# Block products in the last MLP half, Silu gates, and work moved to GpSimd, in a clustered-attention and MLP kernel

## The chip, the core and the metric

The kernel runs on one core of a Trainium2 chip. A core has five engines, each with its own instruction queue that runs in order: TensorE (PE, matmuls and the loading of their weights), VectorE (DVE), ScalarE (ACT), GpSimd (POOL) and SyncE (SP, which issues DMAs here). They meet through semaphores. SBUF is the working memory; TensorE writes to PSUM, eight banks of 2 KB in each of 128 partitions, from where DVE or ACT take the results. The metric is the device time of one execution in microseconds (us).

## The reference: what is computed

```
scores = scale * q @ k^T                     # batch 4, heads 8, 768 tokens, head_dim 64
mask   = argmax(q_n @ c_n^T) == argmax(k_n @ c_n^T)    # 16 clusters per head
attn   = softmax(where(mask, scores, -1e9))
x      = (attn @ v), heads side by side      # 3072 tokens x 512
h      = x @ w_in                            # 512 -> 2048 features
out    = (h * sigmoid(h)) @ w_out            # 2048 -> 512
```

Every query and key gets the cluster whose centroid it points to most. A query sees only the keys of its own cluster. The result goes through an MLP with Silu gate.

## The kernel before

**Attention.** For one head a *job* holds six tiles of 128 queries and six of 128 keys. `load` fetches them as f32 (tile `raw`), `hi` (lines 123 to 127) rounds 128 times the value to f16, `lo` (L132) gives the rest as a second f16 half; the two stand side by side in `hl`. `xpose` turns them by DMA into `ab`, 64 rows high half and 64 rows low half. `logits_n` (L180) multiplies by the centroids into PSUM, `lsum` (L192) adds the two halves into an SBUF tile `L` that has two buffers, `mx_n` (L208) takes the largest of 16 clusters, and `ge_n` (L217) compares: the one-hot code. For the *late* jobs (heads 16 to 31 of 32) `c_scale` (L224, L225) makes of the ones 16384 on the queries' side, and of the zeros -16384 on the keys' side, on GpSimd. `c_xpose` and `c_move` (L237) bring the code by two DMAs into rows of `ab` below the high half, so that one matmul (`qk_mm`, L354) gives score and mask at once. `exp` (L359) makes the weights `P` on ACT. `pv` (L371) multiplies them with `vt` (values with a column of 2.0, whose sum serves for the division and halves the result), `norm` (L381, L383) divides, and the result is turned into `xt`, features by tokens.

**MLP.** Half a batch (384 tokens, named `(b, c)`) has 16 feature tiles. `unit_a` (L421) is four matmuls of 128 by 384; the result `ph` is h/2. ACT takes `tn = tanh(ph)` (L441) and DVE `gt = (tn + 1) * ph` (L444), which is h times sigmoid(h). After the last exp, `unit_a2` does two tiles at once (L467, L468) in the PSUM banks ("halls") that the scores used. The second matrix is applied either by `part_b` (L480) or, for pairs of token tiles, by class `Pair`: a two-by-two block multiplication with seven products in place of eight (L561), after four sums of activations (`sums`, L544) and with sums of weights made once (L514). Its results are put together out of PSUM (L567 to L604) and stored.

**Order.** The work up to about 38 us is a list written out by hand (`plan`). Behind it a planner in the same file runs: it keeps a clock for each engine with a length for every piece, and issues on each engine the piece that is next by due time. For TensorE it ranks scores, values, feature tiles and products; the rate of the scores is set by `PACE`, `LEAST`, `LESS`, `GAIN`. Dates count scores: `SPLIT` says at which score a head's split falls due, `AHEAD`, `VALUES` and `CAST` when its loads and its cast (L295) do. The planner only sets the order in the queues; on the chip, the semaphores decide. There are 192 scores (units); the last is number 191.

## Time and profile before

| | us |
|---|---|
| three runs: lowest, median, highest | 298.30, 299.58, 299.75 |
| profiled execution: first to last instruction (span) | 297.1 |
| PE, PEld, DVE busy | 288.0, 203.4, 219.7 |
| ACT, POOL busy | 221.7, 72.3 |

The profile gives the span of the one execution it recorded; that execution's own device time is not among its numbers, and the runs' median stands 2.5 us above the span. Busy time counts instructions on the engine, not the issuing of DMAs. Matmuls are pipelined and their ends are modelled, so a busy TensorE need not be one at its best. In the groups by line, the numbers behind the bar are busy us, mean ns of one, then the idle time of the engine just before and what ended it.

### The profile page before, as it was taken

The numbers are of one execution on the slowest core, as the hardware profiler recorded it, in microseconds if no ns is written. First come the engines' busy times: TensorE is split into PE (matmuls) and PEld (weight loads), VectorE is DVE, ScalarE is ACT, GpSimd is POOL, SyncE is SP. The second block draws the span as 40 slices with busy tenths as digits, with TensorE's granted clock in tenths as the row PEclk, the third lists the DMA queues.
The fourth block names the chain that finished last, engine by engine and source line by source line (L and its number), as shares of the span: only waits on it lengthen the run. The fifth ranks groups of instructions, "written<-read, shape, count | busy, mean of one in ns | idle before, by whom it ended". The sixth has DMA issues, their size and how long they took to land.

```text
span 297.1 us, 8186 instructions
## 1 busy us (share of the span) xinstructions
PE 288.0 (97%) x3273; PEld 203.4 (68%) x3273; DVE 219.7 (74%) x459; ACT 221.7 (75%) x365; POOL 72.3 (24%) x133
## 2 busy tenths in 40 slices
PE   7899799999999999999999999999999999999995
PEld 3786666566766566667766776678767786767783
DVE  5998559586897799997797766997664553569743
ACT  5899689765896579988579668997798879845410
POOL 2889510001031023544232560243200000000000
PEclk9999999999999999999999999999999999999999
DMA  6689999999866599999877979785220020110113
GB/s 208 206 244 204 158 257 228 170 235 185 242 128 174 133 214 227 209 223 196 232 175 144 196 215 226 170 126 119 74 57 17 13 86 15 49 38 0 35 38 141
DMA packets 77220, 44.61 MB, mean 150 GB/s; under 512 B 56288, under 2 KB 73088, under 8 KB 77184
## 3 DMA queue, kind: packets, MB, share of 16 engines
q1 hardware_dynamic: 71952, 35.55, 51.7%
q0 software_dynamic: 4800, 8.13, 15.0%
q8 instruction: 25, 0.41, 0.6%
q10 hardware_dynamic: 432, 0.43, 0.4%
q14 instruction: 11, 0.09, 0.1%
HBM read 27.30 MB, written 6.29 MB: 113 GB/s over the span
## 4 chain that ended last, share of the span: by engine, by line
PE 85%; DMA 7%; POOL 2%; DVE 2%; issue 1%; ACT 1%; SPq 0%; POOLq 0%; DVEq 0%; ACTq 0%
PE ph L421 28%; PE pS L354 18%; PE po L561 16%; PE pO L371 10%; PE po L480 9%; DMA raw<-in_q_dram 3%; PE psN L180 3%; DMA ab<-cd 3%; DMA ab<-cdt 1%; POOL hl L125 1%; DVE hl L132 1%; DVE ab L166 1%; POOL vt L295 1%; POOL win_s L613 0%; PE px L393 0%
## 5 line engine op out<-in xcount | busy, mean ns | idle before, releaser
L359 ACT ACTIVATE P<-pS 128x768 f16<-128x768 f32 x192 | 156.9, 826 | 36.9 <-PE pS L354 36.0
L421 PE MATMUL ph<-xt,win_s 128*128 128x384 f16 x512 | 97.6, 326 | 0.0
L354 PE MATMUL pS<-ab 128*128 128x384 f16 x384 | 93.2, 326 | 2.2 <-DMA ab<-cd 1.5
L444 DVE SCALAR_TENSOR_TENSOR gt<-tn,ph 128x384 f16<-128x384 f32 x110 | 58.7, 550 | 21.0 <-ACT tn L441 20.4
L421 PEld LDWEIGHTS <-win_s 128*128 128x128 f16 x512 | 49.3, 98 | 31.1
L441 ACT ACTIVATE tn<-ph 128x384 f32<-128x384 f32 x110 | 55.1, 514 | 3.3 <-PE ph L421 2.4
L354 PEld LDWEIGHTS <-ab 128*128 128x128 f16 x384 | 34.5, 98 | 20.8 <-issue 2.5
L371 PEld LDWEIGHTS <-P 128*128 128x128 f16 x1152 | 39.7, 97 | 5.0 <-DVE ab L166 0.9
L371 PE MATMUL pO<-vt,P 128*128 128x65 f16 x1152 | 41.2, 193 | 0.3 <-DVE ab L166 0.3
L132 DVE SCALAR_TENSOR_TENSOR hl<-raw,hl 128x768 f16<-128x768 f32 (+3 forms) x35 | 32.8, 939 | 1.2 <-POOL hl L125 0.5
L561 PEld LDWEIGHTS <-gt 128*128 128x128 f16 x304 | 29.3, 98 | 5.9 <-DVE gt L544 0.4
L480 PE MATMUL po<-wout_s,gt 128*128 128x512 f16 x128 | 32.5, 379 | 0.0
L295 POOL CAST vt<-vn 128x384 f16<-128x384 f32 x32 | 18.8, 598 | 56.2 <-DMA vn<-in_v_dram 40.7
L561 PE MATMUL po<-wout_s,gt 128*128 128x256 f16 x192 | 24.4, 273 | 0.0
L224 POOL TENSOR_SCALAR od<-od 128x96 f16<-128x96 f16 x16 | 9.3, 580 | 53.3 <-DVE od L217 53.2
L381 DVE RECIPROCAL zr<-pO 128x6 f32<-128x6 f32 x32 | 6.2, 193 | 18.9 <-PE pO L371 18.8
L180 PEld LDWEIGHTS <-ab 128*128 128x128 f16 x458 | 17.3, 97 | 4.0 <-DVE ab L166 0.3
L480 PEld LDWEIGHTS <-gt 128*128 128x128 f16 x128 | 12.0, 98 | 10.6
L383 DVE TENSOR_TENSOR xn<-pO,zr 128x384 f16<-128x384 f32 x32 | 17.8, 557 | 1.1
L180 PE MATMUL psN<-stk,ab 128*128 128x32 f16 (+1 forms) x458 | 18.6, 188 | 0.0
L561 PE MATMUL po<-tw,sg 128*128 128x256 f16 x128 | 16.3, 273 | 0.0
L192 DVE TENSOR_REDUCE L<-psN 128x192 f32<-128x384 f32 (+1 forms) x27 | 14.8, 549 | 1.9 <-PE psN L180 1.7
(101 smaller groups left out, 259.0 us busy)
## 6 DMA issues: line engine op xcount, KB each, us to landing
raw<-in_k_dram SPq DMA_DIRECT2D x31, 192.0 KB, 4.0
out_dram<-ot SPq DMA_DIRECT2D x23, 256.0 KB, 2.4
raw<-in_q_dram SPq DMA_DIRECT2D x24, 192.0 KB, 3.9
vn<-in_v_dram SPq DMA_DIRECT2D x16, 192.0 KB, 4.2
vn<-in_v_dram POOLq DMA_DIRECT2D x16, 192.0 KB, 4.3
win_s<-in_moe_w_in_dram POOLq DMA_DIRECT2D x8, 256.0 KB, 6.2
wout_s<-in_moe_w_out_dram POOLq DMA_DIRECT2D x4, 512.0 KB, 18.8
raw<-in_q_dram SPq DMA_DIRECT2D x2, 384.0 KB, 4.2
```

The costliest lines, as they stand in the source:

```text
L132: nc.vector.scalar_tensor_tensor(out=hl[:, s, 1, :], in0=raws[job.name][:, s, :], scalar=QS, in1=hl[:, s, 0, :], op0=ALU.mult, op1=ALU.sub ...
L180: nc.tensor.matmul(L[:, n % g, :, n // g], ab[:, i, :], stk[:, job.groups[i // 3][0], x : x + w], start=(x == 0), stop=(x + w == 2 * HC),)
L295: nc.gpsimd.tensor_copy(vt[:, :, 0:D], vns.pop(i))
L354: nc.tensor.matmul(pS[:, e, 0:HALF], abs_[kj.name][:, kn, :], rhs, start=True, stop=True)
L359: nc.scalar.activation(out=P, in_=pst.pop(u)[:, :, 0:HALF], func=AF.Exp, bias=0.0, scale=ESC)
L371: nc.tensor.matmul(o[:, (2 * t + h) * VW : (2 * t + h + 1) * VW], Ps[i + h, c, j // 2][:, j % 2, ts(t, 128)], vtb[(i + h) % 13][:, j, 0:VW ...
L383: nc.vector.tensor_tensor(out=xn, in0=ov[:, :, 0:D], in1=zr.unsqueeze(2).to_broadcast([128, 2 * NM, D]), op=ALU.mult)
L421: nc.tensor.matmul(ph[:, 0:HALF], win_s[:, r, ts(fb, 128)], xts[b, c][:, r, :], start=(r == 0), stop=(r == NR - 1))
L441: nc.scalar.activation(out=tn, in_=ph[:, 0:HALF], func=AF.Tanh, bias=0.0, scale=1.0)
L444: nc.vector.scalar_tensor_tensor(out=gt[:, fb, :], in0=tn, scalar=1.0, in1=ph[:, 0:HALF], op0=ALU.add, op1=ALU.mult)
L480: nc.tensor.matmul(po, gts[b, c][:, fc, ts(t, 128)], wout_s[:, fc, :], start=(fc == 0), stop=(fc == NFB - 1))
L561: nc.tensor.matmul(o, l[:, f, :], x, start=(f == 0 and k in begins), stop=(f == HK - 1), skip_group_check=True)
```

## The change

1. Of batch 3's two halves, the feature tiles 8 to 15 are no longer computed by `unit_a` but as two blocks of four tiles (class `Quad`), each by seven block products of four 192-column matmuls. Four sums of tokens per half (`x_sum`, DVE) and eight sums of weights (`t_piece`, GpSimd or DVE) go before; two copies out of PSUM (`copy`) and four additions (`plus`) go between the products of a block.
2. Behind the last exp, ACT loads the table of Silu. From there the gate is one Silu on ACT, without DVE.
3. For ten heads (`BY_GP`) `hi` runs on GpSimd rather than on DVE or ACT.
4. For late jobs the comparison is a subtraction on GpSimd, in place in `L`, and `c_scale` compares with zero and scales in one.
5. The last two pairs get two sum tiles more (`OWN`), so that the third and fourth sum no longer overwrite the activations.
6. New dates and pace constants, and rules for the order of the blocks among the plain tiles.

```diff
-        nc.vector.tensor_tensor(
-            out=ohv(job), in0=Ls.pop(job.name), in1=mx.unsqueeze(2).to_broadcast([128, g, HC, m]), op=ALU.is_ge
-        )
+        mx = mx.unsqueeze(2).to_broadcast([128, g, HC, m])
+        if job.late:
+            nc.gpsimd.tensor_tensor(out=Ls[job.name], in0=Ls[job.name], in1=mx, op=ALU.subtract)
+        else:
+            nc.vector.tensor_tensor(out=ohv(job), in0=Ls.pop(job.name), in1=mx, op=ALU.is_ge)
...
-        o = ohv(job)
-        nc.gpsimd.tensor_scalar(out=o[:, :, :, 0:3], in0=o[:, :, :, 0:3], scalar1=OHV, scalar2=None, op0=ALU.mult)
-        nc.gpsimd.tensor_scalar(
-            out=o[:, :, :, 3:6], in0=o[:, :, :, 3:6], scalar1=OHV, scalar2=-OHV, op0=ALU.mult, op1=ALU.add
-        )
+        o, d = ohv(job), Ls.pop(job.name)
+        nc.gpsimd.tensor_scalar(out=o[:, :, :, 0:3], in0=d[:, :, :, 0:3], scalar1=0.0, scalar2=OHV, op0=ALU.is_ge, op1=ALU.mult)
+        nc.gpsimd.tensor_scalar(out=o[:, :, :, 3:6], in0=d[:, :, :, 3:6], scalar1=0.0, scalar2=-OHV, op0=ALU.is_lt, op1=ALU.mult)
...
+        tn = None if silu_on else mp.tile([128, HALF], f32, name="tn", bufs=4)
 
         def tanh():
+            if silu_on:
+                nc.scalar.activation(out=gt[:, fb, :], in_=ph[:, 0:HALF], func=AF.Silu, bias=0.0, scale=2.0)
+                done(ph)
+                act.gate = None
+                return
...
+        def tanh():
+            if silu_on:
+                nc.scalar.activation(out=gt[:, fb : fb + 2, :], in_=ph[:, :, 0:HALF], func=AF.Silu, bias=0.0, scale=2.0)
+                act.gate = None
+                return
+            nc.scalar.activation(out=tn, in_=ph[:, :, 0:HALF], func=AF.Tanh, bias=0.0, scale=1.0)
...
-                self.s1, self.s2 = (mp.tile([128, HK, 128], f16, name="sg", tag=x, bufs=1) for x in self.sgs)
-            s1, s2, a11, a12, a21, a22 = self.s1, self.s2, self.r1(0), self.r1(1), self.r2(0), self.r2(1)
+                self.s = [mp.tile([128, HK, 128], f16, name="sg", tag=x, bufs=1) for x in self.sgs]
+                if len(self.s) == 2:
+                    self.s += [self.r2(0), self.r1(1)]
+            (s1, s2, s3, s4), a11, a12, a21, a22 = self.s, self.r1(0), self.r1(1), self.r2(0), self.r2(1)
             o, x, y, op = (
-                (s1, a21, a22, ALU.add), (s2, s1, a11, ALU.subtract), (a21, a11, a21, ALU.subtract), (a12, a12, s2, ALU.subtract)
+                (s1, a21, a22, ALU.add), (s2, s1, a11, ALU.subtract), (s3, a11, a21, ALU.subtract), (s4, a12, s2, ALU.subtract)
...
+    QUADS = {(3, 0): (2, 3), (3, 1): (2, 3)}
+    ORDERS = {(3, 0): [0, 5, 1, 2, 3, 7, 103, 6, 4, 102], (3, 1): [2, 3, 1, 6, 4, 102, 103, 0, 7, 5]}
+    HT = HALF // 2
+    tsl, xss = {}, {}
...
+    def t_piece(s, r, e, v):
+        TV[0] = v
+        a, b_, op = (
+            (wblk(2 + r, 1), wblk(r, 1), ALU.subtract), (t_at_(0, r), wblk(r, 0), ALU.add),
+            (wblk(2 + r, 0), t_at_(1, r), ALU.subtract), (wblk(r, 1), wblk(r, 0), ALU.subtract),
+        )[s]
+        (nc.gpsimd if e == "P" else nc.vector).tensor_tensor(out=t_at_(s, r), in0=a, in1=b_, op=op)
...
+        lo_, up = slice(0, HT), slice(HT, HALF)
+        a11, a12, a21, a22 = xt[:, 0:2, lo_], xt[:, 2:4, lo_], xt[:, 0:2, up], xt[:, 2:4, up]
+        a, b_, op = (
+            (a21, a22, ALU.add), (z[:, 0], a11, ALU.subtract), (a11, a21, ALU.subtract), (a12, z[:, 1], ALU.subtract),
+        )[k - 1]
+        nc.vector.tensor_tensor(out=z[:, k - 1], in0=a, in1=b_, op=op)
...
+    silu_on = []
+
+    def gating(h, o, after):
+        def tanh():
+            if silu_on:
+                nc.scalar.activation(out=o, in_=h, func=AF.Silu, bias=0.0, scale=2.0)
+                after()
+                return
...
+            def gate(eng):
+                if eng == "P":
+                    nc.gpsimd.tensor_tensor(out=tn, in0=tn, in1=h, op=ALU.mult)
+                    nc.gpsimd.tensor_tensor(out=o, in0=tn, in1=h, op=ALU.add)
+                else:
+                    nc.vector.scalar_tensor_tensor(out=o, in0=tn, scalar=1.0, in1=h, op0=ALU.add, op1=ALU.mult)
...
+        def product(self, k):
...
+            o = self.Y if k in (2, 5, 3) else self.A
+            for j in range(2):
+                for r in range(2):
+                    f = 4 * n + (2 if k == 3 else 0) + j
+                    if k in (1, 2, 3):
+                        w = win_s[:, r + (0 if k == 1 else 2), ts(f, 128)]
+                    else:
+                        w = t_at_({7: 0, 6: 1, 4: 2, 5: 3}[k], r, n // 2)[:, n % 2, ts(j, 128)]
+                    if k in (1, 2, 4):
+                        x = xt[:, r + (0 if k == 1 else 2), HT * (k == 4) : HT * (k == 4) + HT]
+                    else:
+                        x = z[:, {5: 0, 6: 1, 7: 2, 3: 3}[k], r, :]
+                    nc.tensor.matmul(
+                        o[:, HT * j : HT * j + HT], w, x,
+                        start=(k in (1, 2, 5, 3) and j == 0 and r == 0), stop=(r == 1), skip_group_check=True,
+                    )
...
+        def copy(self, eng, k):
...
+            nc.vector.tensor_tensor(
+                out=getattr(self, o).rearrange("p j t -> p (j t)"), in0=i, in1=x.rearrange("p j t -> p (j t)"), op=ALU.add
+            )
...
-    PACE, LEAST, LESS, GAIN = 1.37, 23, 13, 0.03
-    HOLD, ROUND, SIDE, LEAD = -7, 8, 4, 11
+    PACE, LEAST, LESS, GAIN = 1.41, 25, 15, 0.05
+    HOLD, ROUND, SIDE, LEAD = -10, 8, 3, 15
     WEIGHTS = 15.5
     ROOM, CODES, TURN, BY_POOL = (1.3, 0.8, 2.0), 1.5, 1.0, 99
-    MARGIN = 0.1
-    EARLY_T = 67
+    BY_GP = [12, 13, 14, 15, 16, 17, 19, 22, 23, 28]
+    MARGIN = -0.05
+    EARLY_T = 60
...
+            def lower(t):
+                add("DVE", t, 0.95 if i in BY_GP else 0.9, lambda: lo(job), turned, 1.5)
+
+            i = int(job.name[1:])
+            if i in BY_GP:
+                add("POOL", t, 2.5, lambda: hi(job, "pool"), lower, 1.5)
+            else:
+                either(t, 0.5, 0.72, lambda e: hi(job, "act" if e == "A" else None), lower, 1.5)
...
+            if job.late:
+                add("POOL", t + 0.06, 0.8, lambda: ge_n(job), codes, 0.2)
+            else:
+                add("DVE", t, 0.33, lambda: ge_n(job), codes, 0.6)
...
-    SPLIT = [27, 27, 33, 41, 43, 44, 51, 56, 67, 72, 79, 80, 81, 83, 84, 87, 99, 102, 105, 122, 124, 132, 135, 142]
-    AHEAD, VALUES, CAST = [9, 8, 10], [1, 0, 4], [7, 3, 12]
+    SPLIT = [29, 37, 26, 44, 42, 46, 50, 52, 66, 73, 74, 75, 69, 86, 81, 85, 99, 105, 107, 122, 123, 133, 126, 133]
+    AHEAD, VALUES, CAST = [13, 6, 7], [0, 1, 2], [6, 0, 13]
...
+            pool = backlog("POOL", t) + POOLT < backlog("DVE", t)
+            eng, length = ("POOL", 1.7) if pool else ("DVE", 0.4)
+            add(eng, t, length, lambda: t_piece(s, r, eng[0], v), lambda t: (t_at.__setitem__((s, r, v), t), t_step(n + 1, t, v)), 1.0)
...
+        if ready_t[0] == B * H - H + 1 and any(n > 1 for x in QUADS.values() for n in x):
+            t_step(0, t, 1)
...
+    date(174, t_start)
...
+    OWN = {(B - 1, 1, "x"): SG["x"] + ("ab10", "ab11"), LAST: ("ab6", "ab7", "ab8", "ab9")}
...
+        if key in OWN:
+            when(key, ("s1", "lo1"), sum_(3, 0.5))
+            when(key, ("s2", "hi1"), sum_(4, 0.5))
...
+            self.q, self.left, self.at, self.asked, self.hall = Quad(b, c, n, hall), [1, 2, 6, 5, 3, 7, 4], {}, set(), hall
...
+            def plus(k, first):
+                if k not in self.asked and all(x in at for x in first):
+                    self.asked.add(k)
+                    add("DVE", max(at[x] for x in first) + 0.15, 0.55, lambda: q.plus(k), lambda t: self.tell(k, t))
+
+            if name == "p1":
+                add("ACT", t + 0.2, 0.45, lambda: q.copy("A", 1), lambda t: self.tell("h0", t))
+            if name == "p5":
+                either(t + 0.2, 0.55, 0.45, lambda e: q.copy(e, 5), lambda t: self.tell("h2", t))
+            plus("c11", ("p2", "h0"))
+            plus("u4", ("p6", "h2"))
+            plus("c12", ("p3", "u4"))
+            plus("c22", ("p7", "u4"))
...
+                add("ACT", t + (0.2 if k == "c21" else 0.1), 0.42 if k == "c21" else 0.46, f, gate)
...
+                def last():
+                    exp(u)
+                    if u == NU - 1:
+                        nc.scalar.preload_act_table(AF.Silu)
+                        silu_on.append(True)
+
+                add("ACT", t + 0.2, 0.75 + (2.0 if u == NU - 1 else 0.0), last, lambda t: exp_at.__setitem__(u, t), 0.2)
```

More of the change, by code (lines that the diff above doesn't have):

```diff
@@ L894, in landed @@
             turn_at[i] = t
+            t_start(t)
             if i in after_turn:
@@ L1165, in unit_piece, with next_, whole @@
-        return then
+            whole(b, c, fb, t)
+        def then(t):
+            def next_(t):
+                if act.gate:
+                    add("DVE", t + 0.1, 0.92 if two else 0.52, act.gate, gated)
+                else:
+                    gated(t)
+            add("ACT", t + 0.2, 0.8 if two else 0.42, act.tanh, next_)
+            end(b, c)
+        return then
+    begun_ = set()
+    def whole(b, c, fb, t):
+        for h, name in enumerate(("lo", "hi")):
+            need = [gate_at.get((b, c, x)) for x in range(h * HK, h * HK + HK)]
+            if h == fb // HK and None not in need:
+                for key, rows in watch.get((b, c), ()):
+                    for x in rows:
+                        tell(key, name + x, max(need))
+                if c == 0 and b in CROSS:
+                    kept(b, h, t)
@@ L1167, in sent, with quad_piece, quad_step @@
+    def quad_piece(hall):
+        b, c, n = qa.pop(0)
+        if hall:
+            halls.pop(0)
+        g = Going(b, c, n - 100, hall)
+        quads.append(g)
+        then = quad_step(g)
+        return lambda t: (then(t), end(b, c))
+    def quad_step(g):
+        k = g.left.pop(0)
+        if not g.left:
+            quads.remove(g)
+        g.q.product(k)
+        return lambda t: g.tell(f"p{k}", t)
     def sent(t):
```

207 lines of the change are left out of this document (167 added, 40 removed).

## The prediction

> **What bounds the kernel now.** I read the page's first part, then the busy time of each engine in stretches of 10 us, then the chain of waits in order of time, and last the groups by line with the shapes kept apart.
>
> ```profile
> PE 288.0 (97%) x3273; PEld 203.4 (68%) x3273; DVE 219.7 (74%) x459; ACT 221.7 (75%) x365; POOL 72.3 (24%) x133
> ```
>
> TensorE is busy 97% of 297.1 us, no other engine over 75%. The average could hide a stage with another limit, so the stretches come next. Their columns are start:end, length, then busy us of PE, weight load, DVE, ACT and POOL with instruction counts, granted clock, DMA share and GB/s.
>
> ```profile
> 0.00:10.00 10.00, 7.70 (x82) 4.33 (x83) 6.81 (x33) 5.80 (x12) 4.24 (x14) 1.00 0.76 227
> ...
> 30.00:40.00 10.00, 8.24 (x125) 6.09 (x123) 4.57 (x13) 6.85 (x11) 4.11 (x8) 1.00 1.03 186
> 40.00:50.00 10.00, 10.00 (x93) 6.40 (x92) 9.40 (x19) 9.57 (x19) 0.70 (x2) 1.00 1.19 247
> ...
> 120.00:130.00 10.00, 10.00 (x141) 7.17 (x140) 9.77 (x21) 9.15 (x17) 4.60 (x10) 1.00 1.14 230
> ...
> 160.00:170.00 10.00, 9.79 (x119) 7.30 (x118) 8.79 (x19) 7.08 (x12) 4.62 (x11) 1.00 0.87 173
> ...
> 220.00:230.00 10.00, 10.00 (x104) 7.26 (x102) 5.86 (x12) 8.86 (x17) 0.00 (x0) 1.00 0.06 12
> ...
> 270.00:280.00 10.00, 10.00 (x75) 7.06 (x73) 8.04 (x13) 4.71 (x7) 0.00 (x0) 1.00 0.00 0
> ...
> 290.00:297.10 7.10, 3.40 (x31) 2.64 (x28) 2.33 (x5) 0.38 (x1) 0.00 (x0) 1.00 0.40 143
> ```
>
> The idle time of TensorE is in three places: before 40 us (the list written out by hand, which the change leaves alone), 3.7 us after the last matmul (copy and store of the last rows, left alone too), and 0.21 us between 160 and 170. Of the 25 stretches from 40 to 290 us the other 24 have 10.00, as the rows of 40 and 270 show it, at full clock. So the time can fall by what TensorE work is removed plus the little that it waits, and it rises by every new wait of TensorE, however idle the engine that causes it. DVE, at 9.4 to 9.8 of 10 in some stretches, is the engine with the least room.
>
> The chain of waits gives what a matmul costs in a full stream (start, us, what, count):
>
> ```profile
> 258.87 1.10 PE pO L371 x36
> 259.97 1.75 PE po L561 x16
> 261.88 6.50 PE ph L421 x40
> 268.38 1.75 PE po L561 x16
> ...
> 271.43 0.87 PE po L561 x8
> ...
> 276.20 0.87 PE po L561 x8
> ...
> 278.38 15.04 PE po L561 x136
> ```
>
> 384 columns (ph) take 6.50/40 = 162.5 ns and 256 columns (po) 1.75/16 = 109.4 ns: 0.415 ns a column and 3.2 ns fixed. The line gives 30.2 ns for 65 columns; the first row has 1.10/36 = 30.6. In the last phase 136 matmuls take 15.04 us where 136 x 109.4 ns is 14.88: 0.16 us of waits.
>
> **The change part by part.** *Seven block products.* Each of the four blocks (tiles 8 to 11 and 12 to 15 of both halves of batch 3) replaces 16 matmuls of 384 columns by 28 of 192. No row has 192; the line gives 82.9 ns. 28 x 82.9 = 2.32 us against 16 x 162.5 = 2.60 us: 0.28 us less a block, **1.1 us less in all**. Bounds: without any fixed cost, 28 x 81.25 ns, 1.3 us less; if 192 columns cost what 256 do, 28 x 109.4 ns, 1.9 us more. I take the line, since the 65-column row, further out than 192, lies on it.
>
> What the products need besides:
>
> ```profile
> L570 DVE TENSOR_TENSOR ot<-po,ot 128x256 f32<-128x256 f32 x8 | 3.4, 420 | 0.7 <-PE po L561 0.4 <-ACT P L359 0.3
> L594 DVE TENSOR_TENSOR ot<-po,uu 128x512 f32<-128x512 f32 x7 | 4.8, 689 | 3.1 <-PE po L561 3.0
> L567 ACT ACTIVATE ot<-po 128x256 f32<-128x256 f32 x8 | 3.1, 392 | 2.2 <-PE po L561 2.0
> L488 ACT ACTIVATE ot<-po 128x512 f32<-128x512 f32 x3 | 1.8, 594 | 2.6 <-PE po L480 2.6
> L514 DVE TENSOR_TENSOR tw<-wout_s,tw 128x512 f16<-128x512 f16 x3 | 1.2, 418 | 0.0
> L125 POOL TENSOR_SCALAR hl<-raw 128x768 f16<-128x768 f32 x2 | 4.3, 2128 | 1.4 <-DMA raw<-in_q_dram 1.4
> L468 DVE SCALAR_TENSOR_TENSOR gt<-tn,ph 128x768 f16<-128x768 f32 x9 | 8.6, 952 | 3.5 <-ACT tn L467 3.4
> ```
>
> Per block two copies out of PSUM, by the ACT rows halfway between 392 and 594, 0.49 us each, and four additions, halfway between 420 and 689, 0.55 us each. In all, 2 us on ACT and 8.9 us on DVE. Eight weight sums of 512 values are 8 x 0.42 = 3.3 us if on DVE; the planner sends them to GpSimd first, which has nothing to do in the stretch from 220 us. No row has that operation there; at the 2.77 ns an element of its split (2128/768) it is 1.4 us each, 11 us one after another, beside other engines' work. Eight token sums of 384 values are at most 8 x 0.42 us. None is on TensorE, but each block is now a chain: a product, a copy, a product, an addition, and so on, seven deep. Its cover is the other TensorE work open at that time. For the last half it is good: from 261.88 us there are eight plain tiles (5.2 us), two blocks that cover each other (4.6 us) and the 32 matmuls of older products that now stand between the tiles (rows from 268.38 to 276.20, 3.5 us). If cover runs out, one hop of a chain is a copy or an addition, about 0.5 us; I take nothing, with two hops in each of the four blocks, 4 us, as upper bound.
>
> *Silu gates after the last exp.* The nine gates of two tiles each, all after 258 us, leave DVE: 8.6 us, against at most 4.5 us of additions in that half. They gain one load of ACT's table:
>
> ```profile
> L647 ACT ACT_TABLE_LOAD x1 | 1.3, 1283 | 1.7 <-PEq L1338 1.7
> 257.19 0.92 ACT L441 ACTIVATE tn<-ph 128x384 f32<-128x384 f32 x2
> 258.91 0.81 ACT L467 ACTIVATE tn<-ph 128x768 f32<-128x768 f32 x1 [0.80 <-PE ph L421]
> 261.92 0.49 ACT L402 ACTIVATE xt<-px 128x384 f16<-128x384 f16 x1 [2.20 <-PE px L393]
> ```
>
> ACT stands idle 0.80 and 2.20 us right where the 1.28 us fall, and TensorE is then at 36 + 16 matmuls that need no gate. Cost nothing; if the cover were gone, 0.5 us (1.28 less 0.80).
>
> *Ten upper splits on GpSimd.*
>
> ```profile
> L127 DVE TENSOR_SCALAR hl<-raw 128x768 f16<-128x768 f32 x21 | 11.7, 562 | 0.0
> L217 DVE TENSOR_TENSOR od<-L,mxn 128x192 f16<-128x192 f32 x16 | 6.0, 376 | 0.4
> L224 POOL TENSOR_SCALAR od<-od 128x96 f16<-128x96 f16 x16 | 9.3, 580 | 53.3 <-DVE od L217 53.2
> ```
>
> Each goes from 0.56 us to 2.13 us: DVE loses 5.6 us, GpSimd gains 21.3 us, each job is 1.6 us later. TensorE sees this only if the job's rows come late for a score; earlier dates stand against it. I take nothing.
>
> *Late comparisons on GpSimd.* Sixteen times 0.376 us leave DVE (6.0 us). On GpSimd 192 values take between 0.53 us (192 x 2.77 ns) and 1.16 us (two of the 96-wide rows). Sixteen codes come 0.2 to 0.8 us later; nothing if hidden.
>
> *Dates, and two more buffers for the last pairs.* They can remove the 0.21 us at 160 and the 0.16 us at the end, or add waits. The wait at 160 is a code that lands late:
>
> ```profile
> 166.94 0.50 PE L354 MATMUL pS<-ab 128*128 128x384 f16 x2 [0.21 <-DMA ab<-cdt]
> ```
>
> Earlier splits speak for its removal, the longer way through GpSimd for more of its kind. I take 0.0, with -0.4 and, for sixteen late codes at 0.2 to 0.3 us, +4 as ends.
>
> Sum: 297.1 - 1.1 = 296.0 us of span. The page has no device time of this one execution; the runs' median of 299.58 us lies 2.5 us above its span (the fastest, 298.3, lies 1.2 above). With the distance of the median kept, 296.0 + 2.5 = **298.5 us**, 0.4% less: under the 0.5% (1.5 us) that I take as what a measurement can tell from no change.
>
> **The rivals.**
> *Faster than told (0.26).* Products and waits both pay: -1.1 -0.4, and the less loaded DVE takes out small waits that no row shows, at most as much again. That is 297.3 to 298.1 us. For it: DVE at 9.77 of 10; against: TensorE does not wait for DVE in those stretches, so there is little to win.
>
> *The logits' buffers (0.18; slower).* The tile of summed logits has two buffers. Before, DVE's own comparison frees it; after, GpSimd does, at the end of its queue.
>
> ```profile
> 118.31 0.56 POOL L237 DMA_DIRECT2D ab<-cdt  x1 [4.91 <-PE ph L421]
> 163.70 0.29 POOL L225 TENSOR_SCALAR od<-od 128x96 f16<-128x96 f16 x1
> 167.83 0.56 DVE L192 TENSOR_REDUCE L<-psN 128x192 f32<-128x384 f32 x1
> ```
>
> The scale at 163.70 ends at 163.99, the reduction two jobs on starts at 167.83: 3.8 us. A split (2.13) and a comparison (0.5 to 1.2) in the queue leave about 1 us, and one wait of GpSimd for its next move, 4.9 us at 118.31, uses it up. Then DVE stands in its reduction, and the gates queued behind it, and the banks that TensorE needs, are late. At 0.3 us for each of sixteen jobs that is 4.8 us: 298.5 + 4.8 = 303.3, at half of that 300.9. It decides for slower from 0.16 us a job (2.6 us, 301.1).
>
> *GpSimd and DVE stand in each other's way (0.06; slower).*
>
> ```profile
> 7.46 3.42 POOL L125 TENSOR_SCALAR hl<-raw 128x576 f16<-128x576 f32 x2 [3.18 <-DMA raw<-in_q_dram]
> 7.57 1.16 DVE L132 SCALAR_TENSOR_TENSOR hl<-raw,hl 128x576 f16<-128x576 f32 x1
> 14.65 0.75 DVE L132 SCALAR_TENSOR_TENSOR hl<-raw,hl 128x576 f16<-128x576 f32 x1
> ```
>
> The lower split takes 0.75 us alone and 1.16 us beside GpSimd's upper split, 0.4 us more. Two such operations in each of ten splits are 8 us of DVE, less than the 11.6 us it gives away. If instead it waited out each split, 21 us, DVE would have 10 us more in stretches that are nearly full; with half of it reaching TensorE, 298.5 + 5 = 303.5 us. The row is against it: the operation started 0.1 us into a split of 1.7 us and was over before that split was. The Trainium skill's page "SBUF — State Buffer" (section "SBUF: two separate sides") holds that the port pair which VectorE and GpSimd share is locked for a whole instruction and the loser fully blocks; by that rule the dearer case would hold. This trace shows a delay of 0.4 us, not a block.
>
> *The products' chain lacks cover (0.10).* The change does not do what it says: two to eight hops of 0.5 us give the 1.1 us back and more, 299.5 to 302.5.
>
> **How the numbers follow.** The forecast (0.40) reaches from 297.9 to 299.0. Of it I give 0.07 to faster (under 298.08), 0.33 to same. Faster than told: 0.26, all faster. Logits' buffers: 0.18 slower by their price. Port: 0.06 slower. Chain: 0.04 same, 0.06 slower. Sum: faster 0.33, same 0.37, slower 0.30. The range must leave out no more than 0.2: from 297.1 (the fastest case, less 0.2) to 302.6, beyond which lie half of the buffers' case and the port's.
>
> **What the changed profile would show.** 112 matmuls of 192 columns at 83 ns in the stream, and the last matmul about 1.1 us sooner after the same start at 40 us. TensorE at 10.00 in all stretches from 40 to 290. ACT with a second table load of 1.28 us near 257 us and no DVE gate behind it. GpSimd's splits at 2.13 us, its busy time at about 72 + 21 + 10 us. Wrong would be: TensorE under 9.8 in several stretches between 100 and 220, with DVE's reduction of the logits waiting for GpSimd's scale; lower splits of 2 us and more; or gaps of 0.5 us before the products between 230 and 280, released by copies and additions.

## The result and the profile after

The changed kernel takes 303.04 us (median of 6 runs, 301.66 to 303.83), the kernel before 299.53 us (6 runs, 298.30 to 299.75): ratio 1.0131, 95% interval 1.0094 to 1.0169. It is slower by 1.3%, where 298.5 us was forecast, and 303.04 lies above the range. The profiled execution took 301.66 us (span 299.8), the fastest of its six; what follows explains that one, and the median has 1.4 us more that no trace of it shows. The profiled executions of the other kernels below have a device time 1.7 to 1.9 us above their span (2.3 us for two of them). The execution behind the profile of before (span 297.1) was then one of about 299 us, and not of the median's 299.58. Ratios leave out executions in a slower state, among them two of the four of m_quads and one of the ten of p_gpboth below, whose medians have them in.

The page's first part after, and then the busy time in three stretches, first of before, then of after (columns as in the prediction: PE, weight load, DVE, ACT, POOL, clock, DMA share, GB/s):

```profile
PE 289.8 (97%) x3321; PEld 206.8 (69%) x3321; DVE 213.7 (71%) x442; ACT 226.9 (76%) x380; POOL 120.1 (40%) x167
```

```profile
40.00:60.00 20.00, 20.00 (x181) 12.38 (x180) 15.51 (x30) 17.57 (x31) 0.88 (x3) 1.00 1.21 212
60.00:255.00 195.00, 194.79 (x2233) 136.73 (x2232) 149.06 (x300) 156.63 (x256) 46.03 (x91) 1.00 0.70 153
255.00:290.00 35.00, 35.00 (x299) 26.41 (x298) 23.32 (x38) 15.37 (x27) 0.00 (x0) 1.00 0.10 34
```

```profile
40.00:60.00 20.00, 18.77 (x171) 11.21 (x170) 13.49 (x27) 16.49 (x28) 0.96 (x2) 1.00 1.23 211
60.00:255.00 195.00, 193.90 (x2223) 135.71 (x2222) 144.99 (x279) 156.27 (x255) 92.92 (x124) 1.00 0.72 154
255.00:290.00 35.00, 33.85 (x333) 28.14 (x332) 21.11 (x42) 20.31 (x43) 0.00 (x0) 1.00 0.09 31
```

TensorE is still 97% busy and POOL has gone from 72 to 120 us, as meant. But TensorE now stands still in all three stretches (1.2, 1.1 and 1.2 us, against 0.0, 0.2 and 0.0). These rows understate it: a matmul's modelled end lies about 0.16 us behind the start of the next, so each wait shows 0.16 us too short. A second count avoids that: from the start of each matmul to the start of the next, less its length by the line that the prediction found (0.415 ns a column and 3.2 ns; 29 ns for the matmuls of 16 and 32 columns, which follow each other after 25 to 29). What is left over are the waits. So counted, the work of all matmuls went from 282.7 to 281.6 us (1.1 us less, as the line must give), and the waits from 9.3 to 13.4 us; the last matmul starts 3.0 us later. Of the waits, 8.4 and 7.4 us lie ahead of 40 us, where the order is the list written by hand; behind it they go from 0.9 to 6.0 us. "Waits" below always means this count, of the profiled execution; numbers in the brackets of a row are the profile's own.

Where they are: near 45 us, near 110 us, and behind 260 us. The first place, in order of time (start, us, engine, line, operation, and in brackets the idle time before and what ended it):

```profile
45.23 0.56 DVE L127 TENSOR_SCALAR hl<-raw 128x768 f16<-128x768 f32 x1 [1.58 <-DMA raw<-in_k_dram]
47.30 1.25 PE L371 MATMUL pO<-vt,P 128*128 128x65 f16 x36 [0.39 <-DVE gt L449]
49.22 0.81 PE L421 MATMUL ph<-xt,win_s 128*128 128x384 f16 x4 [0.35 <-DVE gt L449]
50.85 0.34 PE L393 MATMUL px<-ident,xn 128*128 128x128 f16 x3 [0.49 <-DVE xn L383]
```

DVE stands 1.58 us for the keys of a job, and its gates (L449) and its division (L383) queue up behind that; TensorE waits for them three times. The job is number 10: the new dates split it first (`SPLIT` begins 29, 37, 26 for jobs 8, 9, 10; before 27, 27, 33), while the list written by hand still loads 8, 9, 10 in that order. The second place is a transposition that lands late, the third are the block products (L715), which wait for their additions (L738) and copies (L728):

```profile
111.89 0.52 PE L180 MATMUL psN<-stk,ab 128*128 128x32 f16 x12 [0.89 <-DMA ab<-hl]
...
258.14 0.48 ACT L728 ACTIVATE hq<-ph 128x384 f32<-128x384 f32 x1
260.18 0.49 PE L715 MATMUL ph<-xt,win_s 128*128 128x192 f16 x4
260.76 0.49 ACT L728 ACTIVATE hq<-ph 128x384 f32<-128x384 f32 x1 [1.36 <-issue]
261.28 0.56 DVE L738 TENSOR_TENSOR hq<-ph,hq 128x384 f32<-128x384 f32 x1
261.89 0.82 PE L715 MATMUL ph<-xs,ts 128*128 128x192 f16 x8 [0.33 <-DVE hq L738]
```

The copy at 260.76 is of product 1, which was long done; ACT stood idle for 1.36 us and the copy started 0.09 us after the end of product 2 at 260.67. Product 2 writes other columns of the same PSUM tile:

```
both = ps.tile([128, 2, 512], f32, name="ph2", tag="st", bufs=2)
self.A, self.Y = both[:, 0, 0:HALF], both[:, 1, 0:HALF]
```

Products 1, 6, 7, 4 go into half A, products 2, 5, 3 into half Y. The program's waits are kept for the tile as a whole: a copy that reads A waits for the product last written into Y, and a product for Y waits for an addition that reads A. The built program of after says so too: in each of its four blocks the copy of product 1 waits for a count of TensorE's semaphore that the last matmul of product 2 brings, and the matmuls of product 1 raise none. The hop is then not a copy or an addition alone, but these and a product more.

### The profile page after: what moved, and what is told of

Read it like the earlier page. It is cut to its first block, busy times and chain, and to the rows that moved or that the text cites. A ratio compares the mean times of both kernels' runs of the same rounds, so it can differ in the third digit from the quotient of the medians.

```text
span 299.8 us, 8326 instructions
## 1 busy us (share of the span) xinstructions
PE 289.8 (97%) x3321; PEld 206.8 (69%) x3321; DVE 213.7 (71%) x442; ACT 226.9 (76%) x380; POOL 120.1 (40%) x167
## 4 chain that ended last, share of the span: by engine, by line
PE 68%; DMA 13%; DVE 8%; POOL 4%; issue 3%; ACT 2%; SPq 1%; DVEq 0%; POOLq 0%; ACTq 0%
PE ph L421 18%; PE pS L354 15%; PE po L574 15%; PE pO L371 8%; DMA raw<-in_k_dram 6%; PE po L492 5%; PE ph L715 3%; PE psN L180 2%; DMA ab<-hl 2%; DMA vn<-in_v_dram 2%; POOL hl L125 2%; DVE hl L132 2%; DMA ab<-cdt 1%; DMA raw<-in_q_dram 1%; DVE gt L449 1%
## 5 line engine op out<-in xcount | busy, mean ns | idle before, releaser
L421 PE MATMUL ph<-xt,win_s 128*128 128x384 f16 x448 | 87.9, 326 | 0.5 <-DVE gt L449 0.3
L449 DVE SCALAR_TENSOR_TENSOR gt<-tn,ph 128x384 f16<-128x384 f32 x101 | 53.9, 550 | 22.6 <-ACT tn L446 21.8
L421 PEld LDWEIGHTS <-win_s 128*128 128x128 f16 x448 | 42.7, 98 | 27.3 <-issue 0.9
L446 ACT ACTIVATE tn<-ph 128x384 f32<-128x384 f32 x101 | 51.5, 518 | 6.7 <-PE ph L421 6.3
L125 POOL TENSOR_SCALAR hl<-raw 128x768 f16<-128x768 f32 (+1 forms) x16 | 33.6, 2103 | 37.7 <-DVE ot L502 12.1
L574 PEld LDWEIGHTS <-gt 128*128 128x128 f16 x272 | 26.4, 98 | 5.1
L295 POOL CAST vt<-vn 128x384 f16<-128x384 f32 x32 | 17.8, 570 | 19.3 <-DMA vn<-in_v_dram 19.1
L574 PE MATMUL po<-wout_s,gt 128*128 128x256 f16 x176 | 22.6, 273 | 0.0
L219 POOL TENSOR_TENSOR L<-L,mxn 128x192 f32<-128x192 f32 x16 | 10.3, 644 | 30.4 <-DVE mxn L208 28.2
L492 PEld LDWEIGHTS <-gt 128*128 128x128 f16 x128 | 12.0, 98 | 10.6
L383 DVE TENSOR_TENSOR xn<-pO,zr 128x384 f16<-128x384 f32 x32 | 17.8, 558 | 1.1
L574 PE MATMUL po<-tw,sg 128*128 128x256 f16 x144 | 18.2, 273 | 0.0
```

Source lines behind the costliest of these rows:

```text
L125: nc.gpsimd.tensor_scalar(out=o, in0=i, scalar1=QS, scalar2=None, op0=ALU.mult)
L295: nc.gpsimd.tensor_copy(vt[:, :, 0:D], vns.pop(i))
L421: nc.tensor.matmul(ph[:, 0:HALF], win_s[:, r, ts(fb, 128)], xts[b, c][:, r, :], start=(r == 0), stop=(r == NR - 1))
L446: nc.scalar.activation(out=tn, in_=ph[:, 0:HALF], func=AF.Tanh, bias=0.0, scale=1.0)
L449: nc.vector.scalar_tensor_tensor(out=gt[:, fb, :], in0=tn, scalar=1.0, in1=ph[:, 0:HALF], op0=ALU.add, op1=ALU.mult)
L492: nc.tensor.matmul(po, gts[b, c][:, fc, ts(t, 128)], wout_s[:, fc, :], start=(fc == 0), stop=(fc == NFB - 1))
```

## The experiments

For all runs side by side: the median, the ratio to the kernel before on the same chip with its 95% interval, and the waits of the profiled execution in three stretches (us). The kernel before itself has medians of 298.6 to 299.5 us on the chips of these runs, so the ratios are to be compared, not the medians.

| kernel | median us | ratio, interval | 40 to 60 | 60 to 255 | from 255 |
|---|---|---|---|---|---|
| before | 299.53 | | 0.0 | 0.8 | 0.1 |
| after | 303.04 | 1.0131, 1.0094 to 1.0169 | 1.9 | 1.8 | 2.3 |
| m_dates | 303.98 | 1.0152, 1.0089 to 1.0216 | 0.3 | 5.4 | 0.7 |
| m_quads | 305.31 | 1.0110, 1.0006 to 1.0214 | 2.8 | 4.5 | 0.7 |
| m_gp | 304.32 | 1.0177, 1.0118 to 1.0235 | 1.5 | 5.5 | 2.3 |
| m_silu | 308.80 | 1.0320, 1.0247 to 1.0393 | 1.7 | 2.7 | 6.3 |
| f_load | 303.58 | 1.0145, 1.0087 to 1.0203 | 0.7 | 5.2 | 2.3 |
| f_load_hop | 303.94 | 1.0134, 1.0056 to 1.0213 | 1.9 | 6.5 | 1.7 |
| p_gpboth | 300.49 | 1.0034, 1.0002 to 1.0066 | 0.5 | 4.2 | 0.1 |
| tail_c1_hop | 301.38 | 1.0063, 1.0022 to 1.0104 | 0.0 | 4.4 | 2.0 |
| f_serial | 302.62 | 1.0103, 1.0051 to 1.0154 | 1.9 | 3.4 | 0.0 |
| tail_serial | 299.78 | 1.0021, 0.9987 to 1.0056 | 0.0 | 5.4 | 0.6 |
| tail_none | 298.66 | 0.9978, 0.9957 to 0.9999 | 0.8 | 2.5 | 0.0 |
| p_dates | 304.85 | 1.0194, 1.0136 to 1.0252 | 3.3 | 3.7 | 1.7 |
| fs_load | 301.84 | 1.0123, 1.0083 to 1.0163 | 1.5 | 6.9 | 0.0 |
| j_8m | 298.81 | 1.0002, 0.9966 to 1.0037 | 1.5 | 2.2 | 0.1 |
| b_nostore | 298.24 | 0.9989, 0.9959 to 1.0018 | 0.6 | 0.6 | 0.1 |
| a_nostore | 301.47 | 1.0113, 1.0081 to 1.0146 | 1.3 | 1.3 | 2.3 |
| fs_vn | 302.22 | 1.0082, 1.0044 to 1.0120 | 0.2 | 7.2 | 0.0 |
| fs_load_nostore | 298.14 | 0.9954, 0.9920 to 0.9987 | 0.6 | 1.0 | 0.0 |

The middle stretch has to be read with care. All instruction queues of f_serial are those of after up to 256 us, and it shows 3.4 us there against 1.8; those of fs_load and f_load are the same up to 259 us, with 6.9 and 5.2 us. tail_none gives every engine the order of before up to the last exp, and yet shows 2.5 us against 0.8, by rows and codes that land late in one execution and not in another. Ahead of 40 us, in no column, the waits lie between 6.1 and 8.4 us.

One profiled execution need not be a typical one: against the medians of their kernels, those of after and fs_load_nostore are 1.4 and 1.7 us short and that of f_serial 2.0, those of fs_load and tail_none 1.7 and 1.8 us long. What rests on the middle column rests on the ratios too.

**One part undone.** m_dates: the old dates, pace constants and turn rule. m_quads: no block products. m_gp: splits and comparisons back on DVE and ACT. m_silu: tanh and DVE's gate to the end.

```diff
 m_dates:  -SPLIT = [29, 37, 26, 44, ...      +SPLIT = [27, 27, 33, 41, ...   (with the other constants)
 m_quads:  -QUADS = {(3, 0): (2, 3), (3, 1): (2, 3)}   +QUADS = {}
 m_gp:     -BY_GP = [12, 13, 14, 15, 16, 17, 19, 22, 23, 28]   +BY_GP = []   (and ge_n, c_scale as before)
 m_silu:   -nc.scalar.preload_act_table(AF.Silu)   -silu_on.append(True)
```

> The changed kernel with the old dates, pace constants and turn rule; products, Silu, GpSimd parts and sum tiles kept. Theory 1 (places): the waits of TensorE at 42 to 52 us (1.9 us over before) and at 110 us (1.05 us) come from the new dates, because DVE stands in front of loads that have not landed; the old dates take them away: 303.0 - 2.9 = 300.1 us. Theory 2 (GpSimd): the splits and comparisons on GpSimd make the codes and splits late whatever the dates: 302.5 us or more.

> The changed kernel with all 16 feature tiles of both halves as plain tiles; all else kept. Theory 1: the chains of the products cost 2.4 us of waits between 260 and 280 us and save 1.2 us of matmuls, so without them it is 1.2 us less, 301.8 us, and TensorE does not wait there. Rival: the chains are covered and the waits there have another cause; then the time rises by the saved matmuls, to 304.2 us, or stays.

> The changed kernel with no upper split and no late comparison on GpSimd; all else kept. Theory 1: they cost TensorE nothing by themselves: 303.0 us within 0.7. Theory 2: they are the main loss: 301 us or less.

> The changed kernel with tanh and the DVE gate to the end, no second table load; all else kept. Theory 1: the Silu gates are neutral: 303.0 us within 0.7. Rival: the 1.28 us of the table load delay the first copies of the products and so start the waits of 260 to 280 us: 302 us or less.

None of the four is clearly faster than the changed kernel. m_dates and m_quads win back the waits of their own part (1.9 to 0.3 us between 40 and 60, 2.3 to 0.7 behind 255) and have as many or more elsewhere. The dates were set for these parts together: the planner's own clock, which knows no late transfer, ends 1.2 us before that of the kernel before with the whole change, but 0.3, 0.6, 1.9 and 3.2 us behind it with one part undone. So an undone part says little of that part here. m_silu is the slowest: without Silu TensorE waits 6.3 us behind 255 us, 3.3 of it ahead of block products and 2.9 ahead of the second matrix. The planner's own clock has it 4.5 us behind the whole change, so in this order the blocks need ACT's gate. m_dates still has all four blocks in the old order of products and waits only 0.7 us behind 255: its planner puts two of them into two separate banks each (tiles `ph` and `py`), where after has all four in shared tiles.

**One part alone, and the order of before kept.** p_gpboth puts the ten splits and the comparisons on GpSimd in the order that the planner made for before. tail_c1_hop and tail_serial keep before's dates and add Silu, the sum tiles, and two or all four blocks (the order of tail_serial leaves that of before at about 235 us, ahead of the last exp); tail_none the same without blocks. p_dates is before with the new dates.

```diff
 p_gpboth:     +hi(job, "pool" if int(job.name[1:]) in (12, 13, 14, 15, 16, 17, 19, 22, 23, 28) else ...)   (and ge_n, c_scale of after)
 tail_c1_hop:  -QUADS = {(3, 0): (2, 3), (3, 1): (2, 3)}   +QUADS = {(3, 1): (2, 3)}   (a product counted ready 0.25 us later)
 tail_none:    +QUADS = {}
 p_dates:      +SPLIT = [29, 37, 26, 44, ...   (and the other constants, nothing else)
```

> The kernel before with the ten upper splits and the late comparisons on GpSimd, with nothing else of the change, the planner's order as before. Theory 1: GpSimd's longer operations cost TensorE little where the order has room: within 1 us of the kernel before. Theory 2 (GpSimd is the main loss, by codes that come late and by DVE's reductions that wait for it): 2 us slower or more, with waits for codes and reductions.

> The kernel before with its dates and its order up to the last part; new are the Silu gates, the additional sum tiles, and the blocks of the last half alone (two blocks, not four), each product counted as ready 0.25 us later. Theory 1 (what was lost is in the dates and in the chains without slack): as fast as before or up to 0.6 us faster (two blocks save 0.56 us of matmuls). Rival: the chains cost more than they save in any order: 0.5 us slower or more.

> Before's dates and order, with Silu gates behind the last exp and the two more sum tiles, and no blocks. If Silu and its table load cost nothing, as the prediction has it: 299.0 to 300.0 us beside 299.5 of before. If the load (1.28 us) and what ACT takes longer reach TensorE: 300.5 us or more, with waits for ACT behind 257 us.

> The kernel before with the new dates and pace constants alone. If the new dates by themselves bring the waits of TensorE between 40 and 230 us (1.9 us near 45 us, and codes and transposes that land late behind that): 301 to 302.5 us. If the dates cost only together with what else was moved: 299.0 to 300.3 us.

p_gpboth is 0.34% slower, about 1 us: the work moved to GpSimd is not free, but it is not the 3.5 us. tail_none, Silu and the two sum tiles alone, is at 0.9978 (0.9957 to 0.9999), the one full kernel here whose interval lies below before. tail_c1_hop waits 2.0 us behind 255 us for two blocks that save 0.56 us, and is 0.6% slower. p_dates is the slowest of these with 1.9%; but the planner's own clock already ends 4.5 us later by it, so it shows that these dates do not suit the old parts, not what they cost in the changed kernel.

**The load order, and the halves.** f_load loads job 10 first in the list written by hand; every queue but that of the loads stays as it was.

```diff
-ce1.A xr0 r8 qk0 ...   w7 r9 xe1.A r10 nm3
+ce1.A xr0 r10 qk0 ...  w7 r8 xe1.A r9 nm3
```

f_load_hop has in addition a product counted ready 0.25 us later. f_serial changes the order of the products in a hall, so that a half is not written while the other is being read, tells the planner that both halves come free together, and counts a product ready 0.05 us later. Its planner then puts one of the four blocks into two separate banks. tail_serial is that order of products with before's dates; there two blocks have separate banks.

```diff
-[1, 2, 6, 5, 3, 7, 4]
+[1, 6, 2, 5, 3, 7, 4] if hall else [1, 2, 6, 5, 3, 7, 4]
...
-            return None if None in need else max(need, default=0.0)
+            return None if None in need else max(need, default=0.0) + 0.05
...
-plus("u4", ("p6", "h2"))
-plus("c12", ("p3", "u4"))
+plus("u4", ("p6", "h2", "p3") if self.hall else ("p6", "h2"))
+plus("c12", ("p3", "u4", "p7") if self.hall else ("p3", "u4"))
```

> The changed kernel, every queue in its order, but the hand-written list loads job 10 first, then 8 and 9 (it had 8, 9, 10). The new dates split job 10 first, and DVE stood 1.58 us in front of its load. Theory 1: with that load three places earlier DVE does not stand there, and of the 1.9 us that TensorE waits between 42 and 52 us at least 1.2 us go: about 301.5 us. Rival: DVE is late there for another cause, or the next load takes the place of this one: 302.5 us or more, the waits still there.

> As the run before, and the planner counts each product of a block as ready 0.25 us later, so that it puts other TensorE work between. Theory 1 (the chains have no slack; every hop is some 0.1 us longer on the chip than planned): the waits between 260 and 280 us fall from 2.4 us to 1 us or less, 1.4 us less than the run before. Rival: the waits there come from missing work, not from missing slack: they stay at 2 us or more.

> The changed kernel, but the products of a plain-tile block go in the order 1, 6, 2, 5, 3, 7, 4, so that no copy or addition reads one half of the PSUM tile while a product is being written into the other half; the planner is told that the tile is released as a whole. Theory (the halves of one PSUM tile hold each other up): TensorE's waits between 255 and 285 us fall from 2.4 us to under 1.0 us, and the time by some 1.4 us, to about 301.6 us beside 299.5 of before. Rival (the chains are simply too short of other work): the waits there stay at 2 us or more, and the time at about 303.

> Before's dates and order up to the last exp, then Silu gates, the two more sum tiles, and all four blocks in the order 1, 6, 2, 5, 3, 7, 4. If the loss is made by the new order ahead of the last exp and by the held-up halves behind it: waits of TensorE from 40 to 257 us as before (under 1.5 us), under 1 us behind it, 298.3 to 299.3 us, so 0.1 to 0.4% under before. If the blocks' chains lack cover in any order: 2 us or more of waits behind 257 us, and 300.5 to 302 us.

f_serial, the busy time in the three stretches:

```profile
40.00:60.00 20.00, 18.63 (x171) 11.29 (x170) 13.31 (x26) 16.39 (x28) 0.96 (x2) 1.00 1.21 216
60.00:255.00 195.00, 192.75 (x2211) 134.51 (x2210) 143.67 (x279) 155.53 (x253) 92.42 (x124) 1.00 0.73 153
255.00:290.00 35.00, 35.00 (x354) 30.07 (x352) 21.49 (x43) 21.05 (x46) 0.00 (x0) 1.00 0.10 34
```

35.00 of 35.00 behind 255 us with all four blocks in place, three of them in shared tiles: the blocks have cover enough, once the order respects what the tile allows. The three later kernels with this order of products (fs_load, fs_vn, fs_load_nostore) do not wait there either. More slack alone is no cure: f_load_hop still waits 1.7 us there, between its two expectations. Of the expected 1.4 us the median shows 0.8 by the ratios (1.0131 to 1.0103), and the intervals overlap. tail_serial has 0.6 us there (one product that waits for an addition) and comes out the same as before.

f_load takes 1.2 us out near 45 us, but its time does not fall. In none of the five kernels with this load order does DVE stand for job 10. In two of them, though, TensorE waits in the same place for something else, the last of `w_in` (1.5 us in f_load_hop, 1.2 in fs_load):

```profile
43.04 0.55 DVE L127 TENSOR_SCALAR hl<-raw 128x768 f16<-128x768 f32 x1
43.99 0.34 PE L421 MATMUL ph<-xt,win_s 128*128 128x384 f16 x1 [1.17 <-DMA win_s<-in_moe_w_in_dram]
```

The second place is near 110 us. f_load's matmuls there, beside those of after (above, 0.89 us):

```profile
110.17 0.81 PE L421 MATMUL ph<-xt,win_s 128*128 128x384 f16 x4
113.89 0.52 PE L180 MATMUL psN<-stk,ab 128*128 128x32 f16 x12 [2.91 <-DMA ab<-hl]
```

The transposed rows were issued at 104.55 us in both. Issues around it (KB each, and the middle of the times from issue to landing in us), first of after, then of f_load:

```profile
vn<-in_v_dram POOLq DMA_DIRECT2D x2, 192.0 KB, 6.5
out_dram<-ot SPq DMA_DIRECT2D x1, 256.0 KB, 3.0
ab<-hl SPq DMA_TRANSPOSE x1, 7.3
```

```profile
vn<-in_v_dram POOLq DMA_DIRECT2D x2, 192.0 KB, 5.6
out_dram<-ot SPq DMA_DIRECT2D x1, 256.0 KB, 3.0
ab<-hl SPq DMA_TRANSPOSE x1, 9.3
```

In after, GpSimd issues its two loads of values 1.1 us behind the transposition, in f_load it issues the first 0.05 us ahead of it, and the transposition lands 2.0 us later. So it is in the other traces that have these queues and the stores: near 110 us TensorE waits 1.0 us in after and f_serial, with the old load order, and 2.0 to 3.1 us in f_load, f_load_hop and fs_load, with the new one. What f_load saves at 45 us is given back there.

**Both mends, and the transfers.** fs_load has both mends, the load order and the order of the products; so have fs_vn and fs_load_nostore. fs_vn lets SyncE issue the sixteen late loads of values. b_nostore, a_nostore and fs_load_nostore leave out the stores of batches 0 to 2 in before, after and fs_load. j_8m moves one date of before by one score.

```diff
 fs_vn:    -lambda: load_v(i, nc.gpsimd)   +lambda: load_v(i, nc.sync)
 *nostore: +if b == B - 1:   (ahead of the stores in part_b and Pair)
 j_8m:     -SPLIT = [27, 27, 33, 41, 43, 44, 51, 56, 67, ...   +SPLIT = [27, 27, 33, 41, 43, 44, 51, 56, 66, ...
```

> The changed kernel with both mends: job 10 loaded first in the list written by hand, and the block products in the order 1, 6, 2, 5, 3, 7, 4. If these two causes are the loss: waits of TensorE of 1.9 and 2.4 us shrink to under 1.2 us together, and the time goes from 303.0 to 300.0 us, half a us from before. If the loss lies in late transposes and codes all over the stretch from 60 to 230 us: 302 us or more, with 3 us or more of waits there.

> The kernel before with one date moved by one score: the split of job 16 at score 66 in place of 67. The planner's own clock ends 0.4 us later by it, and the order behind that place is another on every engine. If any newly made order costs what the chip adds to the planner's clock: 301 to 303 us, with 2 us or more of new waits for transposes, codes or gates behind 60 us. If the loss is the change's own: 299.5 to 300.3 us.

> The kernel before without the stores of batches 0 to 2 (4.7 MB that aren't written, so three quarters of the output are missing). If the DMA engines, near full between 40 and 200 us, cost the kernel before little: 298.7 to 299.5 us, waits behind 40 us from 1.4 to about 1.0 us.

> The changed kernel without the stores of batches 0 to 2 (three quarters of the output are missing). If the full DMA engines make its late transposes and codes: the waits for DMA between 60 and 230 us go from 1.7 us to under 0.5 us and the time falls by 1.2 us or more, to 301.8 us or less, clearly more than the kernel before gains by the same. If the late ones are late by their place in the order: the time falls no more than that of the kernel before, 302.3 us or more.

> The changed kernel with both mends, and the sixteen late loads of values issued by SyncE in place of GpSimd. If the loads on GpSimd's queue make the transposed rows late at 110 us and that gives back what the mends save: the wait there falls from 2.9 us to under 1 us, and the time from 301.8 to 300 us or less, with a before of 299. If the rows are late by all the transfers around them: 2 us or more stay, and 301.5 us or more.

> The changed kernel with both mends, without the stores of batches 0 to 2 (three quarters of the output are missing). If the wait at 110 us is one for full DMA engines and gives back what the mends save: it falls from 2.9 us to under 1 us and the time to 299.5 us or less, where the kernel before without the stores has 298.2. If TensorE's waits move on to the next late transfer: 300.5 us or more, with the 2 us at other places between 60 and 230 us.

j_8m, whose order differs from before's on every engine from about 98 us at the latest, takes the same time (1.0002). So it is not that any newly made order loses. fs_load has no wait behind 255 us, but 6.9 us between 60 and 255, 2.9 of it at 110:

```profile
109.85 0.81 PE L421 MATMUL ph<-xt,win_s 128*128 128x384 f16 x4
113.36 0.82 PE L180 MATMUL psN<-stk,ab 128*128 128x32 f16 x12 [2.70 <-DMA ab<-hl]
```

The median shows nothing of the expected 3 us (1.0123). With the loads of values on SyncE (fs_vn) the wait at 110 us shrinks to 0.3 us, as expected, but others take its place (1.2 us at 138 for transposed rows, 2.0 us at 157 for a gate of DVE), and 1.0082 with an interval that overlaps is no clear gain. Without the stores, the same order of all other instructions gives another time. fs_load_nostore near 110 us, and in the three stretches:

```profile
109.53 0.52 PE L180 MATMUL psN<-stk,ab 128*128 128x32 f16 x12 [0.57 <-DMA ab<-hl]
```

```profile
40.00:60.00 20.00, 19.73 (x192) 12.10 (x190) 13.30 (x26) 16.85 (x29) 0.96 (x2) 1.00 1.23 214
60.00:255.00 195.00, 194.43 (x2223) 136.43 (x2220) 145.08 (x279) 157.75 (x257) 92.98 (x124) 1.00 0.66 132
255.00:290.00 35.00, 35.00 (x361) 30.79 (x359) 23.26 (x46) 17.20 (x41) 0.00 (x0) 1.00 0.08 30
```

Its waits behind 40 us are 1.6 us (in the shortest of its eleven executions), and its ratio is 0.9954 (0.9920 to 0.9987), 1.7% below that of fs_load, with intervals far apart. The same stores cost before 0.1% (b_nostore, within its error) and the unmended kernel 0.2% (a_nostore against after, overlapping; it still waits 1.3 us near 45 us and 2.3 us behind 255). So with the stores the two mends gain nothing that the ratios show (1.0131 to 1.0123), and without them 1.6%, some 4.7 us (1.0113 to 0.9954, intervals apart). That is the plainest sign that the load order and the halves, which wait 4.2 us in after, are causes of the loss, and that transfers that land late take the gain away again while the stores run. Either mend alone without the stores was not run. With all three gone the changed kernel is 0.35% below before without stores (0.9954 / 0.9989), about the 1.1 us of work that the products save, but that is within the two intervals: a gain over before is not shown.

Left open: why the order of the changed kernel suffers so much more from the late transfers than that of before. The DMA share between 60 and 255 us is nearly the same (0.72 and 0.70). The order around single transfers plays a part, as at 110 us; that the planner left its new order less time to spare fits, but was not tested, and the stores were tested only as a whole.

## Why the prediction was wrong

Two terms that the sum took as nothing failed: the cover of the blocks' chains (2.3 us of waits) and the dates (1.9 us near 45 us, and late rows further on). The work on GpSimd cost about 1 us more. Part by part:

- *Seven block products: right.* The 112 matmuls of 192 columns cost what the line gave. The chain of waits after has `256.08 0.66 PE ph L715 x8`, 82.5 ns a matmul, against 82.9 from the line.
- *The cover of the chains, "I take nothing": wrong, 2.3 us.* The upper bound of 4 us held it; the value taken did not. I counted the other TensorE work beside the blocks, which was enough (f_serial: no wait), but not what the program lets a product wait for: two halves of one PSUM tile count as one tile. (The copies' 2 us on ACT were a slip in the working, eight times 0.49 us are 3.9; ACT has 3.4 us in seven.)
- *Silu, "cost nothing": right.* tail_none, which has the sum tiles too, is 0.2% faster. The table load is there, and the next gate follows at once:

```profile
255.64 0.80 ACT L359 ACTIVATE P<-pS 128x768 f16<-128x768 f32 x1
256.46 1.28 ACT L1571 ACT_TABLE_LOAD   x1
257.75 0.49 ACT L442 ACTIVATE gt<-ph 128x384 f16<-128x384 f32 x1
```

  The Trainium skill's page "ScalarE: Activation LUTs" (section "What ACT_TABLE_LOAD costs") gives 1283 ns for the load, as here, and about 1380 ns of drain beside it. These rows show no drain: 0.01 us lie between the load and the next gate, and the last exp ended 0.02 us ahead of the load (255.64 + 0.80).

- *Splits and comparisons on GpSimd, "I take nothing": mis-sized by about 1 us* (p_gpboth, 0.02 to 0.66%). The durations were right (2.13 us and 0.53 to 1.16 us forecast); POOL's 120 us, where about 103 were forecast, have the eight weight sums besides (9.1 us) and scales that now compare as well, 23.5 us in place of 15.7:

```profile
L125 POOL TENSOR_SCALAR hl<-raw 128x768 f16<-128x768 f32 x12 | 26.5, 2209 | 34.2 <-DVE ot L502 12.1 <-DMA raw<-in_k_dram 10.5 <-DVE gt L449 8.1
L219 POOL TENSOR_TENSOR L<-L,mxn 128x192 f32<-128x192 f32 x16 | 10.3, 644 | 30.4 <-DVE mxn L208 28.2 <-DVE zr L381 2.1
```

- *The dates, "0.0, with -0.4 and +4 as ends": the other step that failed.* The change's own diff gave it away: `SPLIT` 29, 37, 26 against loads of jobs 8, 9, 10 in that order by hand. The prediction looked for late codes at 160 us, where the waits were before, and did not follow the new dates to their loads. That alone is 1.9 us of waits; the late rows further on come to that (1.0 us at 110 us in after), and how much of those is the dates' and how much GpSimd's was not separated.
- *Rival, the logits' buffers: not seen.* DVE's reduction never waits for GpSimd; all its idle time is TensorE's logits:

```profile
L192 DVE TENSOR_REDUCE L<-psN 128x192 f32<-128x384 f32 x26 | 14.4, 552 | 5.7 <-PE psN L180 5.7
```

- *Rival, the port: not seen at its price.* The lower splits take 1013 ns where they took 990, and the one that lies longest inside a split of GpSimd is delayed, not blocked:

```profile
L132 DVE SCALAR_TENSOR_TENSOR hl<-raw,hl 128x768 f16<-128x768 f32 x26 | 26.1, 1013 | 0.3
...
175.44 2.33 POOL L125 TENSOR_SCALAR hl<-raw 128x768 f16<-128x768 f32 x1
175.81 1.46 DVE L132 SCALAR_TENSOR_TENSOR hl<-raw,hl 128x768 f16<-128x768 f32 x1
```

It begins 0.37 us into the split and is over 0.5 us before it, 0.5 us longer than the 0.96 us that it takes with GpSimd idle; p_gpboth has two more that lie wholly inside a split, of 1.58 and 1.46 us. By the rule of the Trainium skill's page "SBUF — State Buffer" (section "SBUF: two separate sides"), that the loser fully blocks, it could not have ended first; the trace disagrees here as it did before.

- *Rival, the chain lacks cover (0.10): right in place and price* (2.3 us; two to eight hops of 0.5 us were forecast), wrong in its reason: other work was there (f_serial). It comes on top of the dates; that several causes add up, none of the rivals had.
- *The sum* was set 2.5 us above the span, while an execution of after stands 1.8 to 1.9 us above its own. That is 0.6 to 0.7 us, and small here.

## What to carry to other kernels

When dates move, follow each moved piece to the transfer that feeds it, also through lists written by hand: an instruction that waits for it holds up all that is queued behind it on its engine. Give what must overlap in PSUM tiles of its own, or an order that allows for one shared tile; "other work is there" is no cover for a wait that the program itself puts in. One mended wait can be given back at the next transfer that lands late, and one part undone makes a new order, so several causes have to be taken away together before one of them is called harmless.

## What the runs showed of the hardware

The same transposition of one job, issued at 101.5 to 105.2 us, took the longer to land, the closer behind it GpSimd issued its next load of values:

| run | first load of values after the transposition's issue, us | us to landing |
|---|---|---|
| after, f_serial | 1.1 | 7.3, 7.2 |
| fs_load_nostore | 0.7 | 8.0 |
| f_load_hop | 0.5 | 8.2 |
| f_load, fs_load | 0.05 and 0.07 ahead of it | 9.3, 9.1 |

In the changed kernel the transpositions of a job issued between 40 and 200 us land after 3.8 to 12.1 us. The table is of this one place; whether the place in the queues does it, or what else is in flight then, was not separated.
